# Top-k attention and a SwiGLU block on one core: the penalty of the scores left out comes from ScalarE's Relu instead of VectorE's comparison

## The chip, the core and the metric

The kernel runs on one core of a Trainium2 chip. The metric is device time in microseconds (us) of one execution; lower is better. Five engines work side by side, each in the order of its own queue: TensorE (PE; its weight loads are listed as PEld), VectorE (DVE), ScalarE (ACT), GpSimd (POOL) and SyncE (SP, which issues the DMAs here). An engine that meets an instruction whose input is not there waits, and everything behind it in its queue waits too.

## The reference, cut to what matters

```python
# q, k, v: 8 batches x 8 heads x 576 x 64
scores = scale * np.matmul(q, k.transpose(0, 1, 3, 2))
kth = np.partition(scores, -32, axis=-1)[..., -32:-31]
scores = np.where(scores >= kth, scores, -1000000000.0)
attn = np.exp(scores - scores.max(-1, keepdims=True))
attn = attn / (attn.sum(-1, keepdims=True) + 1e-09)
x = (attn @ v)                      # then to 4608 tokens x 512
g = x @ w_gate                      # 512 -> 1536
out = (g * sigmoid(g) * (x @ w_val)) @ w_out
```

Each row of 576 scores keeps its 32 largest; the others get a weight of zero. Everything is float32.

## The kernel before, in words

**Units.** The attention is cut into 160 units, one for a batch, a block of queries and a pair of heads. Of a batch's five query blocks, four have 128 rows, and their units hold two heads as two halves of 576 columns (128 such units in all). The fifth has 64 rows, and its units pack both heads into one 128-row tile of 576 columns (32 "half units", four in a row at the end of each batch).

**What a unit goes through.** `scores` (L278): PE multiplies queries and keys into PSUM banks (four for a full unit, two for a half one; L308, L294), and ACT copies them to the tile `sc` (L313, L299). `select` (L316): DVE finds the 32 largest of each row with four `max` of eight each into `m` (L328) and three `match_replace` that take the found ones out (L332, working copy `e`). Then DVE writes the penalty into `e`: 0 where the score is at least the 32nd largest, -3e38 elsewhere (L338). `penalize` (L342): POOL computes `bias` from the row's largest (L348) and adds `sc` to the penalty in `e` (L350). `weigh` (L353): ACT takes the exponential of `e` with its row sums (L359), and adds a small constant to them (L364). `normalize` (L367): DVE takes the reciprocal of the sums (L371), ACT multiplies (L374). `turn` (L376): PE transposes `e` through PSUM (L386), ACT copies it to `et` (L387). `values` (L397): PE multiplies with v (L420), ACT copies into the block `xT` (L436).

**The second half.** Each 256 tokens whose `xT` is complete make a block of `feed` (L462; 18 blocks): PE products with the gate and value weights (L476); ACT applies tanh, a scaling and a shift, or copies (L501 to L503, L508); POOL multiplies (L504, L509). The output product is done in seven quarter products (L562), fed by sums and differences that POOL forms (L569, L577, L582, L610) and collected by ACT copies (L589, L596, L639, L651) and POOL adds (L548). Block 0 uses a plain product (L522). The weights are rounded on the way in by ACT, DVE and POOL (L114 to L123) in the first fifth of the span.

**The order of the work.** It is written out by hand in one loop over the units (L747), and each engine keeps it: L818 to L830 tie every instruction to the one before it on its engine. In round n of the loop, in this order: ACT work left over from `feed`; `penalize(n-1)`; POOL work left over; the ACT part of `normalize(n-2)`; `scores` of unit n+1 (even rounds only, which do two units' scores); `values` of two units (even rounds); the matmuls of the second `scores`; `weigh(n-1)`; the copies of the second `scores`; then `select(n)` on DVE, with pieces of `feed` on PE, `turn(n-2)` and the preparation of later batches' keys and queries (L248) between its steps; at its end the reciprocal of `normalize(n-1)`. How many pieces of `feed` a round gets is fixed when the program is built, by a budget of 7.0 (later 6.4) per full unit less a charge for the other matmuls (`share`, L694).

```python
        flush(on_act)
        if 0 <= n - 1 < NU:
            penalize(n - 1)
        flush(on_pool)
        run(scaled)
        if nxt:
            run(nxt.pop(0))
```

**Buffers.** `sc` and `e` have three buffers, `m` two. The PSUM pool for scores, transposes and value products has five banks (`ps_t`, L86), so that the second scores of an even round need the banks of the first; `feed` has three (`ps_f`).

Of the kernel before, what the change touches and what calls it, by code (L numbers as in the profile page):

```python
# [8 lines left out]
AF = mybir.ActivationFunctionType  # L9
ALU = mybir.AluOpType  # L10
FP32 = mybir.dt.float32
# [4 lines left out]
P = 128  # L16
TOP_K = 32
LOWEST = -3.4028234663852886e38
FAR = -3.0e38
EPS = 1.0e-9  # L20
BLK = 256
WP = 256
# [3 lines left out]
def kernel(  # L26
# [37 lines left out]
    nc = tc.nc  # L64
# [11 lines left out]
    scale = 1.0 / float(D) ** 0.5  # L76
# [6 lines left out]
    small = ctx.enter_context(tc.tile_pool(name="small", bufs=3))  # L83
# [190 lines left out]
    def n_heads(qt):  # L274

        return 1 if qt == J else 2
# [39 lines left out]
    def select(n):  # L316

        nh = n_heads(units[n][1])
        sc = state[n]["sc"]
        m = small.tile([P, 2, TOP_K], FP32, tag="m", name="m", bufs=2)  # L320
        heads = [slice(t * S, (t + 1) * S) for t in range(nh)]
        e = work.tile([P, 2 * S], FP32, tag="e", name="e", bufs=3)
        state[n] |= dict(m=m, e=e, heads=heads)
        cur = sc
        rounds = TOP_K // 8
        for r in range(rounds):
            for t, hs in enumerate(heads):
                nc.vector.max(m[:, t, 8 * r : 8 * r + 8], cur[:, hs])  # L328
                yield
            if r < rounds - 1:  # L330
                for t, hs in enumerate(heads):
                    nc.vector.match_replace(  # L332
                        e[:, hs], m[:, t, 8 * r : 8 * r + 8], cur[:, hs], LOWEST
                    )
                    yield
                cur = e
        for t, hs in enumerate(heads):
            nc.vector.tensor_scalar(  # L338
                e[:, hs], sc[:, hs], m[:, t, TOP_K - 1 : TOP_K], FAR, ALU.is_lt, ALU.mult
            )  # L340

    def penalize(n):  # L342

        st = state[n]
        sc, m, e, heads = st.pop("sc"), st.pop("m"), st["e"], st["heads"]
        nh = len(heads)
        bias = small.tile([P, 2], FP32, tag="bias", name="bias")
        nc.gpsimd.tensor_scalar_mul(bias[:, 0:nh], m[:, 0:nh, 0], -scale)  # L348
        for hs in heads:
            nc.gpsimd.tensor_tensor(e[:, hs], e[:, hs], sc[:, hs], ALU.add)  # L350
        st["bias"] = bias

    def weigh(n):  # L353
# [393 lines left out]
    for n in range(NU + 3):  # L747
        nh = n_heads(units[n][1]) if n < NU else 1
        topk = select(n) if n < NU else no
        norm = normalize(n - 1) if 0 <= n - 1 < NU else no  # L750
        nxt = [scores(m) for m in scored(n)]
# [16 lines left out]
        if 0 <= n - 1 < NU:  # L768
            penalize(n - 1)
# [90 lines left out]
```

## Time and profile before

| | |
|---|---|
| three runs | 1786.62, 1790.91, 1791.84 us; median 1790.91 |
| the profiled execution | 1790.76 us, of it a span of 1788.7 us from the first to the last instruction |
| mean granted TensorE clock | 0.966 of full speed |
| instructions | 30860 |

The profile's page gives for each engine its busy time and the number of its instructions, then the same in 40 equal slices of the span as tenths (one slice is 44.7 us), then groups of instructions: line, engine, operation, output and inputs with shapes, count, then the busy time of the group, the mean ns of one, and the idle time just before them with what ended it. Views of the trace give the same for any stretch, instruction by instruction (timeline), or as sums by stretch (windows).

### The profile page before, as it was taken

How to read it: one execution, taken by the hardware profiler on the slowest of the kernel's cores; microseconds unless marked ns; L12 is line 12 of the kernel's file. 1: busy time of each engine (PE TensorE's matmuls, PEld its weight loads, DVE VectorE, ACT ScalarE, POOL GpSimd, SP SyncE). 2: the span in 40 equal slices, each digit the busy share in tenths (PEclk: the TensorE clock that was granted, in tenths of full speed). 3: DMA queues.
4: the chain of work that ended last, by engine and by line, in shares of the span. 5: the costliest groups of instructions: out<-in, count | busy, mean ns of one | idle time of the engine just before them, and what ended most of it. 6: DMA issues, size and time to landing. Idle time of an engine off the chain costs nothing.

```text
span 1788.7 us, 30860 instructions
## 1 busy us (share of the span) xinstructions
PE 1686.3 (94%) x11012; PEld 1396.2 (78%) x11012; DVE 1619.7 (91%) x3372; ACT 1209.5 (68%) x2881; POOL 1068.0 (60%) x1058
## 2 busy tenths in 40 slices
PE   4458999799999999999999999999999999999999
PEld 3337678588888888888888878888888878888877
DVE  7999999999999999999999989999999999999400
ACT  6788776667667677667666776767676776676431
POOL 4878856455565646564656646566556555756434
PEclk7669999899999999999999999999999999999989
DMA  7433030001200030001200030000300020000000
GB/s 193 126 96 95 32 75 14 13 1 36 60 1 13 3 80 15 12 1 35 62 13 1 13 71 26 1 13 6 90 1 13 1 55 15 13 1 13 1 12 12
DMA packets 109306, 59.67 MB, mean 33 GB/s; under 512 B 88544, under 2 KB 96992, under 8 KB 109152
## 3 DMA queue, kind: packets, MB, share of 16 engines
q1 hardware_dynamic: 108016, 57.37, 12.3%
q8 instruction: 87, 1.43, 0.3%
q14 instruction: 67, 0.55, 0.1%
q10 hardware_dynamic: 1136, 0.33, 0.1%
HBM read 48.23 MB, written 9.44 MB: 32 GB/s over the span
## 4 chain that ended last, share of the span: by engine, by line
PE 81%; DVE 9%; POOL 4%; ACT 3%; issue 2%; DMA 0%; SPq 0%; POOLq 0%; ACTq 0%; DVEq 0%
PE f L476 39%; PE x_ps L562 9%; PE av L420 8%; PE s L308 7%; PE etps L386 6%; PE y_ps L562 6%; DVE m L328 4%; DVE e L332 4%; PE s L294 2%; POOL e L350 1%; PE kqps L263 1%; PE o_ps L522 1%; DVE e L338 1%; DVE size L121 1%; ACT e L359 1%
## 5 line engine op out<-in xcount | busy, mean ns | idle before, releaser
L328 DVE MAX8 m<-e 128x8 f32<-128x576 f32 x864 | 614.5, 746 | 3.3
L350 POOL TENSOR_TENSOR e<-e,sc 128x576 f32<-128x576 f32 x288 | 408.7, 1437 | 111.8 <-DVE e L338 53.8
L332 DVE MATCH_REPLACE8 e<-m,e 128x576 f32<-128x576 f32 x576 | 423.3, 741 | 0.0
L476 PE MATMUL f<-xT,wg 128*128 128x256 f32 x1728 | 405.6, 384 | 0.0
L476 PE MATMUL f<-xT,wv 128*128 128x256 f32 x1728 | 399.6, 380 | 0.0
L476 PEld LDWEIGHTS f<-xT,wg 128*128 128x128 f32 x1728 | 326.4, 192 | 52.2 <-issue 8.9
L476 PEld LDWEIGHTS f<-xT,wv 128*128 128x128 f32 x1728 | 323.0, 190 | 49.1 <-issue 7.9
L504 POOL TENSOR_TENSOR h<-h,half_g 128x512 f32<-128x512 f32 x108 | 139.0, 1287 | 284.1 <-ACT h L503 274.5
L359 ACT ACTIVATE e<-e,bias 128x576 f32<-128x576 f32 x288 | 222.8, 778 | 79.0 <-POOL e L350 79.0
L509 POOL TENSOR_TENSOR h<-h,val 128x512 f32<-128x512 f32 x108 | 139.4, 1291 | 148.7 <-ACT val L508 147.9
L386 PE MATMUL etps<-ident,e 128*128 128x128 f32 (+1 forms) x1312 | 184.0, 284 | 45.7 <-ACT e L374 37.5
L374 ACT ACTIVATE e<-e,tot 128x576 f32<-128x576 f32 x288 | 210.9, 781 | 20.9 <-DVE tot L371 20.8
L308 PE MATMUL s<-kqT 64*128 64x288 f32 x1024 | 181.4, 461 | 41.9 <-ACT sc L313 27.6
L386 PEld LDWEIGHTS etps<-ident,e 128*128 128x128 f32 (+1 forms) x1312 | 157.5, 145 | 76.6 <-ACT e L374 41.4
L387 ACT COPY et<-etps 128x512 f32<-128x512 f32 (+1 forms) x448 | 182.5, 483 | 44.1 <-PE etps L386 44.0
L332 DVE MATCH_REPLACE8 e<-m,sc 128x576 f32<-128x576 f32 x288 | 211.5, 740 | 0.0
L328 DVE MAX8 m<-sc 128x8 f32<-128x576 f32 x288 | 202.5, 739 | 9.1 <-ACT sc L313 9.1
L338 DVE TENSOR_SCALAR e<-sc,m 128x576 f32<-128x576 f32 x288 | 185.4, 680 | 1.1
L313 ACT COPY sc<-s 128x288 f32<-128x288 f32 x512 | 164.9, 407 | 17.0 <-PE s L308 16.8
L308 PEld LDWEIGHTS s<-kqT 64*128 64x128 f32 x1024 | 102.6, 198 | 89.6 <-ACT sc L313 33.0
L420 PE MATMUL av<-et,v 128*64 128x128 f32 (+1 forms) x2560 | 158.6, 267 | 0.0
L501 ACT ACTIVATE h<-f 128x512 f32<-128x512 f32 x108 | 64.3, 595 | 116.8 <-PE f L476 116.6
(73 smaller groups left out, 2045.9 us busy)
## 6 DMA issues: line engine op xcount, KB each, us to landing
v<-in_v_dram SPq DMA_DIRECT2D x32, 256.0 KB, 3.2
kq_in<-in_k_dram SPq DMA_DIRECT2D x63, 128.0 KB, 2.9
kq_in<-in_q_dram SPq DMA_DIRECT2D x63, 128.0 KB, 3.1
w<-in_moe_w_gate_dram SPq DMA_DIRECT2D x12, 512.0 KB, 3.9
w<-in_moe_w_val_dram SPq DMA_DIRECT2D x12, 512.0 KB, 3.7
w<-in_moe_w_out_dram SPq DMA_DIRECT2D x12, 512.0 KB, 3.6
out_dram<-o SPq DMA_DIRECT2D x38, 128.0 KB, 2.4
out_dram<-o SPq DMA_DIRECT2D x16, 256.0 KB, 2.4
```

Source lines behind the costliest of these rows:

```text
L308: nc.tensor.matmul(ps[:, 0:half], slab[d, q0 : q0 + P], slab[d, k0 : k0 + half])
L328: nc.vector.max(m[:, t, 8 * r : 8 * r + 8], cur[:, hs])
L332: nc.vector.match_replace(e[:, hs], m[:, t, 8 * r : 8 * r + 8], cur[:, hs], LOWEST)
L338: nc.vector.tensor_scalar(e[:, hs], sc[:, hs], m[:, t, TOP_K - 1 : TOP_K], FAR, ALU.is_lt, ALU.mult)
L350: nc.gpsimd.tensor_tensor(e[:, hs], e[:, hs], sc[:, hs], ALU.add)
L359: nc.scalar.activation(e[:, hs], e[:, hs], AF.Exp, bias=bias[:, t : t + 1], scale=scale, accum_out=tot[:, t : t + 1],)
L374: nc.scalar.mul(e[:, hs], e[:, hs], tot[:, t : t + 1])
L386: nc.tensor.transpose(ps[0:kl, c * P : (c + 1) * P], e[:, k0 : k0 + kl], ident[:])
L387: nc.scalar.copy(et[0:kl, c0 : c0 + cn, :], ps[0:kl, 0 : cn * P].rearrange("p (c j) -> p c j", c=cn),)
L420: nc.tensor.matmul(av[d, i, 0:ql], weights_, moving, start=c == (0 if last else J), stop=c == (J if last else J - 1),)
L476: nc.tensor.matmul(ps[:, i, :], w[:, kc, m * P : (m + 1) * P], x[:, kc, :], start=(kc == 0), stop=(kc == KC - 1),)
L562: nc.tensor.matmul(ps, lhsT, T[i][m], start=m == 0, stop=m == MQ - 1)
```

## The change

`select` no longer writes the penalty. `penalize` now has ACT scale the 32nd largest by 2^110 into a small tile `top`, compute `Relu(-2^110 * score + top)` into `e` for each head (0 for the scores kept, a very large number for the others), and has POOL subtract that from the scores. The subtraction of a huge number takes the place of the addition of -3e38.

```diff
-FAR = -3.0e38
+BIG = 2.0**110
...
                 cur = e
-        for t, hs in enumerate(heads):
-            nc.vector.tensor_scalar(
-                e[:, hs], sc[:, hs], m[:, t, TOP_K - 1 : TOP_K], FAR, ALU.is_lt, ALU.mult
-            )
 
     def penalize(n):
...
         nh = len(heads)
+        top = small.tile([P, 2], FP32, tag="top", name="top")
+        nc.scalar.mul(top[:, 0:nh], m[:, 0:nh, TOP_K - 1], BIG)
         bias = small.tile([P, 2], FP32, tag="bias", name="bias")
         nc.gpsimd.tensor_scalar_mul(bias[:, 0:nh], m[:, 0:nh, 0], -scale)
-        for hs in heads:
-            nc.gpsimd.tensor_tensor(e[:, hs], e[:, hs], sc[:, hs], ALU.add)
+        for t, hs in enumerate(heads):
+            nc.scalar.activation(
+                e[:, hs], sc[:, hs], AF.Relu, bias=top[:, t : t + 1], scale=-BIG
+            )
+            nc.gpsimd.tensor_tensor(e[:, hs], sc[:, hs], e[:, hs], ALU.subtract)
         st["bias"] = bias
```

## The prediction

> **What bounds the kernel now.** I read the page's busy shares first, then the slices, then the windows by stage.
>
> ```profile
> PE 1686.3 (94%) x11012; PEld 1396.2 (78%) x11012; DVE 1619.7 (91%) x3372; ACT 1209.5 (68%) x2881; POOL 1068.0 (60%) x1058
> ...
> PE   4458999799999999999999999999999999999999
> ...
> DVE  7999999999999999999999989999999999999400
> ```
>
> Two engines look full. The slices part them: in the first four (to 180 us) DVE is full and PE half idle; after that both are full; at the end DVE is done and PE still works. So the windows decide (columns: the stretch, its length, busy us and count of PE, PEld, DVE, ACT, POOL, then granted clock, DMA share, GB/s):
>
> ```profile
> 45.00:90.00 45.00, 21.72 (x138) 15.90 (x138) 45.00 (x92) 34.75 (x76) 37.12 (x31) 0.61 0.44 125
> 90.00:135.00 45.00, 23.57 (x147) 16.25 (x143) 45.00 (x93) 35.60 (x80) 34.80 (x29) 0.63 0.34 95
> ...
> 320.00:500.00 180.00, 168.29 (x1142) 138.77 (x1141) 176.24 (x376) 123.87 (x307) 95.05 (x97) 0.96 0.11 27
> 500.00:800.00 300.00, 298.71 (x1995) 252.09 (x1995) 294.60 (x617) 210.05 (x505) 184.94 (x188) 1.00 0.07 19
> ...
> 1100.00:1400.00 300.00, 298.39 (x1984) 250.57 (x1982) 289.57 (x610) 207.29 (x499) 177.20 (x179) 1.00 0.08 20
> ```
>
> From 500 us on PE is busy 99.5% of the time and DVE 97 to 98%: PE is the bound, with DVE close behind. Only two stretches wait for DVE: the start, and 328 to 355 us, where the second half has no finished tokens and PE stands idle for 11.5 us (sum of its five gaps in the timeline there). PE's work is not touched by the change. So most of what DVE saves cannot shorten the span, but each wait that ACT or POOL puts on PE after 180 us lengthens it at once.
>
> **What is removed.** The groups (count, then busy us and mean ns of one, then idle before):
>
> ```profile
> L350 POOL TENSOR_TENSOR e<-e,sc 128x576 f32<-128x576 f32 x288 | 408.7, 1437 | 111.8 <-DVE e L338 53.8
> ...
> L359 ACT ACTIVATE e<-e,bias 128x576 f32<-128x576 f32 x288 | 222.8, 778 | 79.0 <-POOL e L350 79.0
> ...
> L374 ACT ACTIVATE e<-e,tot 128x576 f32<-128x576 f32 x288 | 210.9, 781 | 20.9 <-DVE tot L371 20.8
> ...
> L338 DVE TENSOR_SCALAR e<-sc,m 128x576 f32<-128x576 f32 x288 | 185.4, 680 | 1.1
> ```
>
> L338 goes: 288 instructions, 185.4 us of DVE. A pair that nothing disturbs takes 0.93 us (timeline at 906 and 916 us), so a full unit of DVE falls from 10.6 to 9.6 us, while PE needs 11.2 (a pair of rounds repeats every 22.4 us). Single ones range from 490 to 1611 ns with a median of 512. The Trainium skill, "SBUF — State Buffer", section Who interferes with whom, says that a VectorE `tensor_scalar` in a two-port mode and GpSimd lock each other out; the spread of L338 fits, and by it POOL would win back something too. The rows bound that: L350 has a mean of 1437 ns and a minimum of 1396, so at most 288 x 41 ns = 12 us of an engine that is 60% busy. I count nothing for it.
>
> **What is added.** No Relu is in the trace. Its nearest row is L374: same shape, same engine, a scale per row; a pair takes 1.44 us. The copy behind it starts about 0.1 us before its end, so 1.34 us of queue. `top` on 128x2 is like L364 (296 ns for 128x2 in the groups by form); Relu reads its result, so all of it counts, with some hand-over. Bounds: 0.2 + 1.34 and 0.3 + 2 x 0.78. I take 1.7 us for a full unit and 1.1 for a half one: 128 x 1.7 + 32 x 1.1 = 253 us of queue, and ACT goes from 1209 to about 1460 us, 82%. The instruction order of the new program holds one table load on ACT, as before, so no reload is added.
>
> The Trainium skill, "ScalarE: Activation LUTs", Rules for kernel authors, speaks against the move: relu and mul belong on VectorE. Its formula (280 ns + 0.833 ns per element with a pointer for the bias) gives 760 ns for one Relu, as L374 has; its rule ignores which engine has room, and by its price the sum below would stay.
>
> **Where it stands.** In round n the new ACT work comes after what `feed` left on ACT and ahead of L374 and the copies of the first scores. Those copies free the PSUM banks in which PE wants to write the second scores. ACT waited for DVE's end at this place already (for the reciprocal), so no wait of a new kind arises on ACT; the 1.7 us are what is new. POOL's L350 now waits for the Relu instead of L338. One even round as it is now:
>
> ```profile
> 918.69 1.24 PE L308 MATMUL s<-kqT 64*128 64x288 f32 x8
> 918.80 0.60 ACT L501 ACTIVATE h<-f 128x512 f32<-128x512 f32 x1 [2.08 <-PE f L476]
> ...
> 919.77 0.63 ACT L503 ACTIVATE h<-h 128x512 f32<-128x512 f32 x1
> ...
> 920.29 1.44 ACT L374 ACTIVATE e<-e,tot 128x576 f32<-128x576 f32 x2
> ...
> 921.62 1.29 ACT L313 COPY sc<-s 128x288 f32<-128x288 f32 x4
> ...
> 922.20 1.07 PEld L308 LDWEIGHTS s<-kqT 64*128 64x128 f32 x8 [0.17 <-ACT sc L313]
> ```
>
> ACT's chain starts when PE ends a product (918.8), so an earlier DVE does not help it. PE reaches the second scores at 922.2 and waits 0.17 us for the first copy. With 1.7 us put in before L374, PE stands still about 1.7 us here, and this comes back whenever the gate's three operations are left over.
>
> **The sum**, from 180 to 1660 us, slack by slack in the timeline:
> - Second scores. Slack is from the end of the first copy to PE's need; ACT's idle time before that copy adds to it, and the last copies trail by 0.2. Of 56 even rounds with two heads, 33 cover 1.7 us; 4 lack 0.6, 10 about 0.8, 2 about 1.4, and 7 the whole 1.7: 2.4 + 8 + 2.8 + 11.9 = 25 us. Of 14 half rounds, 5 lack about 0.25: 1. Together **+26**.
> - Transposes (L386) after L374 in odd rounds. Of 57, 2 have 0.05 us of slack and 10 have 0.75 to 1.0: 2 x 1.65 + 10 x 0.8 = 11; three half ones lack 0.45. **+12**.
> - Half units. From 1044 to 1060.5 us, in three rounds, ACT is busy 14.4 of 16.5 us; 3 x 1.1 more makes 17.7, over the length. That is 1.2 us at least, and some waits stay: 1.5 x 7 batches, **+10**.
> - POOL's L350 now begins at the Relu's end, in places 1.6 to 2.7 us later than now. In three blocks (301, 1066 and 1526 us) the differences of L569 follow it closely, with PE 0.05 us behind; two more lack 0.4. **+7**.
> - The PSUM banks of `feed` have 3.6 us of slack or more between products (L476): nothing. ACT's wait for L350 before the exponentials (57 us from 300 to 1600 us) is mostly filled by the new work; that is why odd rounds cost no more.
> - 328 to 355 us: DVE saves 0.93 us in three rounds, and can come in some 5 us early, from the rounds before, in which PE was the bound. **-8**, between 0 and -18 (11.5 of idle, and half of the 13.7 us at half clock that the clock records show beside it).
> - The start: about 13 units to 180 us. DVE would save 13 x 1.1 = 14. But ACT is busy 66.6 of 80 us between 100 and 180, which is 10.4 of a unit's 12.5; 1.7 more makes 12.1, and it waits 28 us there for weight transfers, 2.1 a unit. If these waits shrink as ACT comes later, there is a gain of 5; if they stay, a loss of 13 x 1.7 = 22. I take **0**, between -14 and +22.
> - Small waits of PE on DVE's or POOL's lateness elsewhere: **-3**.
>
> 26 + 12 + 10 + 7 - 8 - 3 = +44. The sum is made against the profiled execution's 1790.76 us (span 1788.7, 2.1 around it), which lies 0.15 us under the median: **1835 us**.
>
> **Rivals.**
> - *Faster.* DVE's room is used and the covers hold: once DVE leads by up to 5 us, ACT does the Relu in time in which it waits now (it idles 580 us of the span), so that no bank comes late. What is left is the start and the stretch at 328: 14 + 17, **1760 us**. For it: DVE is full to 180 us, and 33 of 56 even rounds have cover. It decides if the waits added stay under the 31 us won. Against it: ACT's chain starts from PE's product, not from DVE.
> - *Nothing to measure* (about 5 us, 0.3%, is what a measurement can tell): losses of some 10 us meet gains of 10, **1791**.
> - *ACT as the bound.* Every even round loses the full amount and the half units saturate: 57 x 1.7 + 16 x 1.1 = 115, less 26, with the start at +22: 44 + 89 + 22, about **1945 us**; half of that already is over 1880. For it: from 860 to 1036 us ACT is busy 120.2 of 176 us, 15.3 of a pair of rounds; 3.4 more makes 84%. Against it: the rounds with 2.4 us of slack, in which ACT waits for PE.
> - That the change does not do what it says can be excluded: the new order has no L338 on DVE.
>
> **How the numbers follow.** Forecast, 1796 to 1880: 0.69. Nothing to measure: 0.08. Faster: 0.14, part of it just under 1785. ACT as the bound, over 1880: 0.09. Faster 0.14, same 0.08, slower 0.78. The range reaches from 1779 to 1880; it leaves out the bulk of the faster case and the last one, some 0.2.
>
> **What would show it.** Right: DVE down by about 185 us with idle time inside, ACT up by about 250; PE idle after 180 us in many gaps of 0.5 to 2 us before the second scores, ended by the copies L313, and before transposes, ended by L374; windows of half units longer by 1 to 2 us. Wrong: PE still at 99% from 500 to 1400 us; or a first stage ending well before 180 us; or PE gaps mainly in places that I gave cover (the products of `feed`).

## The result, and the profile after

| | before | after |
|---|---|---|
| median | 1790.58 us (4 runs, 1786.62 to 1791.84) | 1854.24 us (4 runs, 1852.13 to 1857.83) |
| profiled execution, its span | 1790.76, 1788.7 us | 1854.77, 1853.0 us |
| DVE, ACT, POOL busy | 1619.7, 1209.5, 1068.0 us | 1451.5, 1422.0, 1042.8 us |

The change makes the kernel slower: the ratio is 1.0361, with a 95% interval of 1.0338 to 1.0385, 64 us. The page of after, its busy shares and its PE and DVE slices (a slice is now 46.3 us):

```profile
PE 1706.3 (92%) x11012; PEld 1408.0 (76%) x11012; DVE 1451.5 (78%) x3084; ACT 1422.0 (77%) x3329; POOL 1042.8 (56%) x1058
...
PE   4448999799999999999999999999999999999999
...
DVE  6986788997888978887888878887988879888300
```

DVE has lost its fullness everywhere, the start included, and PE is no fuller for it. The windows of after show where PE lost:

```profile
45.00:90.00 45.00, 23.95 (x144) 16.67 (x141) 41.19 (x87) 39.01 (x87) 33.27 (x28) 0.59 0.40 113
90.00:135.00 45.00, 19.00 (x96) 13.62 (x97) 37.56 (x80) 41.24 (x90) 31.92 (x28) 0.60 0.34 105
...
320.00:500.00 180.00, 164.43 (x1114) 134.67 (x1113) 156.88 (x334) 142.44 (x345) 95.89 (x102) 0.96 0.11 27
500.00:800.00 300.00, 292.79 (x1938) 245.19 (x1937) 255.96 (x545) 240.95 (x566) 167.75 (x174) 1.00 0.08 19
1100.00:1400.00 300.00, 288.80 (x1916) 241.51 (x1917) 250.98 (x536) 236.06 (x564) 164.85 (x173) 0.99 0.10 26
```

From 500 to 800 and from 1100 to 1400 us PE was busy 99.5% and is now busy 97.6 and 96.3%. The granted clock does not account for it: it is 0.99 to 1.00 in these windows, and by the clock records the stretches at half clock after 180 us sum to 27 us in both kernels. In the first stage ACT has taken DVE's part: from 90 to 135 us ACT is busy 41.2 of 45 us, DVE 37.6. The waits of PE in after from 180 to 1720 us (what PE waited for: us in total, times, longest):

```profile
PE s L308 <- ACT sc L313: 21.0, 21, 4.0
PE etps L387 <- ACT e L375: 12.2, 15, 3.4
PE x_ps L563 <- POOL xT L570: 6.7, 3, 2.7
PE s L308 <- ACT et L388: 6.4, 6, 2.3
PE kqps L263 <- ACT et L388: 4.9, 3, 2.0
PE s L294 <- ACT sc L313: 4.1, 2, 2.7
```

In before the same list, over the same stretch, begins:

```profile
PE etps L386 <- ACT e L374: 11.8, 4, 5.3
PE s L308 <- ACT sc L313: 4.3, 2, 3.6
PE x_ps L562 <- POOL xT L569: 2.7, 2, 2.2
```

The places that grew are those that were forecast: score matmuls that wait for the copies, transposes that wait for ACT's multiplication (L374 before, L375 now), the first quarter products behind POOL. For the transposes it is the number of waits that grew (from 4 to 15), not their sum. The even round that the prediction showed, in after:

```profile
957.09 1.24 PE L308 MATMUL s<-kqT 64*128 64x288 f32 x8
...
957.20 0.60 ACT L502 ACTIVATE h<-f 128x512 f32<-128x512 f32 x1 [2.07 <-PE f L477]
...
958.68 0.21 ACT L344 ACTIVATE top<-m 128x2 f32<-128x2 f32 x1
...
958.92 1.44 ACT L348 ACTIVATE e<-sc,top 128x576 f32<-128x576 f32 x2
...
960.27 1.43 ACT L375 ACTIVATE e<-e,tot 128x576 f32<-128x576 f32 x2
...
961.60 1.27 ACT L313 COPY sc<-s 128x288 f32<-128x288 f32 x4
...
962.03 1.19 PEld L308 LDWEIGHTS s<-kqT 64*128 64x128 f32 x8 [1.61 <-ACT sc L313]
```

From `top` to L375 pass 1.59 us (958.68 to 960.27; 1.7 was taken), and the second scores, which had waited 0.17 us, wait 1.61.

**A view made from two traces.** The 11012 matmuls come in the same order in every kernel here. So the k-th matmul's start in one trace, less its start in the trace of before, says how late PE is at each point of the work, and the growth of this between two matmuls says at which line it was lost. This measure is used for all runs below (us; "at 180" is the point that PE passed at 180 us in before; in the 5 us behind that point some runs shift by 1 to 3 us, so these figures are no finer than that):

| | late at 180 us | added from there | at the end |
|---|---|---|---|
| after | +13.1 | +51.1 | +64.2 |

Of the 51.1, the score matmuls L308 hold 29.4, the half units' L294 4.9, the preparation of keys 3.2, the transposes 9.7, the quarter products `x_ps` 6.1; the products of `feed` and the value products come out 1 us shorter each.

### The profile page after: what moved, and what is told of

Its sections match the earlier page's. It is cut to its first block, busy times and chain, and to the rows that moved or that the text cites. A ratio compares the mean times of both kernels' runs of the same rounds, so it can differ in the third digit from the quotient of the medians.

```text
span 1853.0 us, 30964 instructions
## 1 busy us (share of the span) xinstructions
PE 1706.3 (92%) x11012; PEld 1408.0 (76%) x11012; DVE 1451.5 (78%) x3084; ACT 1422.0 (77%) x3329; POOL 1042.8 (56%) x1058
## 4 chain that ended last, share of the span: by engine, by line
PE 72%; ACT 17%; POOL 6%; DVE 1%; issue 1%; DMA 1%; SPq 1%; ACTq 0%; POOLq 0%
PE f L477 36%; PE x_ps L563 9%; PE s L308 6%; PE av L421 6%; PE etps L387 6%; PE y_ps L563 6%; ACT e L348 4%; POOL e L351 3%; ACT e L375 2%; PE s L294 2%; ACT e L360 1%; ACT sc L313 1%; ACT et L388 1%; PE o_ps L523 1%; ACT size L114 1%
## 5 line engine op out<-in xcount | busy, mean ns | idle before, releaser
L351 POOL TENSOR_TENSOR e<-sc,e 128x576 f32<-128x576 f32 x288 | 402.7, 1417 | 345.5 <-ACT e L348 345.5
L360 ACT ACTIVATE e<-e,bias 128x576 f32<-128x576 f32 x288 | 222.8, 779 | 48.9 <-POOL e L351 45.7
L308 PE MATMUL s<-kqT 64*128 64x288 f32 x1024 | 192.2, 470 | 68.6 <-ACT sc L313 49.6
L348 ACT ACTIVATE e<-sc,top 128x576 f32<-128x576 f32 x288 | 209.4, 769 | 5.2
L375 ACT ACTIVATE e<-e,tot 128x576 f32<-128x576 f32 x288 | 206.9, 760 | 0.0
L308 PEld LDWEIGHTS s<-kqT 64*128 64x128 f32 x1024 | 113.9, 200 | 116.6 <-ACT sc L313 58.5
L372 DVE RECIPROCAL tot<-tot 128x2 f32<-128x2 f32 (+1 forms) x160 | 25.0, 156 | 196.8 <-ACT tot L365 196.8
```

The lines of the kernel that those rows point to most:

```text
L308: nc.tensor.matmul(ps[:, 0:half], slab[d, q0 : q0 + P], slab[d, k0 : k0 + half])
L348: nc.scalar.activation(e[:, hs], sc[:, hs], AF.Relu, bias=top[:, t : t + 1], scale=-BIG)
L351: nc.gpsimd.tensor_tensor(e[:, hs], sc[:, hs], e[:, hs], ALU.subtract)
L360: nc.scalar.activation(e[:, hs], e[:, hs], AF.Exp, bias=bias[:, t : t + 1], scale=scale, accum_out=tot[:, t : t + 1],)
L375: nc.scalar.mul(e[:, hs], e[:, hs], tot[:, t : t + 1])
```

## The experiments

The theory: the loss is made by 1.6 us of Relu work a full unit in ScalarE's queue ahead of L374 and the first score copies, and by what stands behind the held subtraction in GpSimd's. The rivals: GpSimd's wait alone; ScalarE's load, wherever it stands. "After" below is the changed kernel, "before" the kernel before; ratios are to runs of before on the same chip. A dash in the diffs is taken out, a plus is put in.

### What VectorE's room is worth alone

```diff
 (before)
-        for t, hs in enumerate(heads):
-            nc.vector.tensor_scalar(
-                e[:, hs], sc[:, hs], m[:, t, TOP_K - 1 : TOP_K], FAR, ALU.is_lt, ALU.mult
-            )
```

> The kernel before without the comparison L338 and with nothing in its place: the penalty is left out, so weights are not limited to the 32 largest; everything else runs as before (POOL still adds sc to e). It shows what VectorE's room alone is worth. Theory (after 180 us PE is the bound, and the change costs time only by the Relu in ScalarE's queue): only the start and the stretch at 328 to 355 us gain, 10 to 25 us, so 1765 to 1780. Rival (VectorE's room is of no use even there, since ScalarE and the weight transfers hold the start): 1785 to 1791.

Measured: 1765.87 us, ratio 0.986 (0.9845 to 0.9875). PE is 14.9 us early at 180 us, gains 5.4 more between 330 and 360 us, and 3.8 near 1060 us. So the room is worth 25 us when nothing is paid for it, and almost nothing of it lies in the stages in which PE is full. That is the ceiling for any change that only takes this comparison off DVE and leaves the order as it is, as against 185 us of removed DVE time.

### The Relu added, nothing removed

```diff
 (before, in penalize)
+        top = small.tile([P, 2], FP32, tag="top", name="top")
+        nc.scalar.mul(top[:, 0:nh], m[:, 0:nh, TOP_K - 1], 2.0**110)
+        for t, hs in enumerate(heads):
+            spare = work.tile([P, S], FP32, tag="spare", name="spare", bufs=1)
+            nc.scalar.activation(
+                spare[:], sc[:, hs], AF.Relu, bias=top[:, t : t + 1], scale=-(2.0**110)
+            )
```

> The kernel before, complete, plus the same scaling and the same Relu on ScalarE in the same place, written to a spare tile that nobody reads; VectorE's comparison and GpSimd's addition stay as they were. Theory (the cost is the 1.6 us a full unit put into ScalarE's queue ahead of L374 and the first score copies): the loss of the change comes back nearly whole without GpSimd being held, 1840 to 1860, with the delay of PE against the kernel before growing at the score matmuls and transposes. Rival (the cost is GpSimd's subtraction, which now waits 345 us for the Relu): no more than 15 us of loss, 1790 to 1806. If VectorE being full adds to it: over 1860.

Measured: 1837.57 us, ratio 1.0264 (1.0244 to 1.0284); PE +3.3 at 180 us, +46.2 from there, of which the score matmuls L308 28.2 and the transposes 13.8, and the quarter products -3.5. It is 2.4 us under the expected range, because the start does not lose 13 us here. After 180 us the Relu in ScalarE's queue makes 46 us here, against the 51 of after, with GpSimd not held (41 in the run that also drops the comparison, below). So GpSimd's wait cannot be the main cause of those.

### The same work, earlier in the queue

```diff
 (after: top and the Relu moved out of penalize into distance)
         next(norm, None)
         scaled = norm
+        if n < NU:
+            distance(n)
         pieces(6)
```

> The changed kernel with the scaling and the Relu of unit n issued on ScalarE at the end of round n, ahead of the last pieces of the second half, instead of at the head of round n+1; GpSimd's subtraction stays where it is. Same work on every engine. Theory (place in the queue): the waits of PE for second scores and transposes after 180 us go, and 35 to 45 of the 54 us lost there come back: 1805 to 1820; the start may stay 13 us late. Rival (ScalarE's load of 77% in total is the cost, wherever it stands): 1845 or more. A new wait could take its place: ScalarE waits for VectorE's end of unit n ahead of the gate's operations; then DVE m is named as releaser of ScalarE's idle time.

Measured: 1823.49 us, ratio 1.0189 (1.0173 to 1.0204); +13.1 at 180 us as in after, +19.8 from there in place of 51.1. At the score matmuls L308 9.5 us are left of 29.4, at the transposes 4.3 of 9.7. ScalarE does the same work, so 31 us of the 51 belong to its place. GpSimd's subtraction is still held here, by 33.4 us from 20 to 180 us against 34.0 in after, and the start loses the same 13.1. The total is 3.5 us over the expected range. ScalarE waits 15.1 us for DVE m before `top` after 180 us: the wait that could take the old one's place is there, and small.

### The same work, later in the queue

```diff
 (after)
         flush(on_act)
-        if 0 <= n - 1 < NU:
-            penalize(n - 1)
         flush(on_pool)
         run(scaled)
         if nxt:
             run(nxt.pop(0))
+        if 0 <= n - 1 < NU:
+            penalize(n - 1)
```

> The changed kernel with the whole of penalize(n-1) moved behind normalize(n-2) and the first scores of the round, so that L374 and the first score copies go ahead of the Relu; GpSimd's subtraction then comes later, and the exponentials wait for it. Same work on every engine. Theory (place in the queue): the second scores and the transposes of odd rounds are free again, some 35 us come back, less a few for exponentials that wait 1 to 2 us a round: 1810 to 1830. Rival (total load): 1845 or more.

Measured: 1899.16 us, ratio 1.0599 (1.0581 to 1.0616); +20.8 at 180 us, +89.6 from there: 45 us worse than after, where a gain of some 30 was expected. Two groups show it, the exponentials (L360) of after and of this run, with the idle time before them at the end of the line:

```profile
L360 ACT ACTIVATE e<-e,bias 128x576 f32<-128x576 f32 x288 | 222.8, 779 | 48.9 <-POOL e L351 45.7
```

```profile
L360 ACT ACTIVATE e<-e,bias 128x576 f32<-128x576 f32 x288 | 223.2, 775 | 196.8 <-POOL e L351 196.2
```

The exponentials now stand right behind the Relu whose subtraction they need, ScalarE sits idle for it in nearly every unit, and everything behind them is late: of the delay added after 180 us, 28.4 us come at the quarter products, 16.0 at the preparation of keys, 16.1 at transposes and 9.8 at value products, most of it at places that lost less or nothing in after. I had put "a few us" on this wait; it is 196 us of ScalarE's time. The run does not yet say whether the place before the copies matters here, so the wait was taken away next.

### The late place without the wait for GpSimd

```diff
 (after's work, GpSimd unheld: before without L338; the Relu to the tile spare in distance)
         if nxt:
             run(nxt.pop(0))
+        if 0 <= n - 1 < NU:
+            distance(n - 1)
```

> As the run with GpSimd unheld (no comparison, the Relu to a spare tile, GpSimd adds sc to e at its old place; the penalty is left out), with the scaling and the Relu moved behind L374 and the first score copies, as in the run with the late Relu. That one lost 108 us where a gain of some 30 was expected; its exponentials waited 179 us for GpSimd. Theory (the wait for GpSimd made that loss; the place behind the copies itself is good): the exponentials no longer wait, and second scores and odd transposes are free: 1775 to 1800, faster than the 1824 of the unheld run with the Relu in front. Rival (ScalarE is too full for the Relu anywhere in the first half of a round): 1824 or more.

Measured: 1782.80 us, ratio 0.9947 (0.993 to 0.9963); PE 8.3 us early at 180 us, +2.9 from there. ScalarE does all of the new work here, 223.4 us of Relu, and the kernel is faster than before. Against the run with VectorE's room alone, which ends at 1765.87 us, the Relu costs 17 us in this place (20 between the two profiled executions, 13.4 of them after 180 us: +2.9 against -10.5). Those 13.4 at most are left for the load as the cause after 180 us. It also lays the loss of the late run on the wait for GpSimd. By which way, this run does not part: the exponentials no longer wait for GpSimd, and GpSimd's own queue, behind which the quarter products stood, no longer waits for the Relu. (It is no usable kernel: the penalty is left out.)

### ScalarE's work in front, GpSimd unheld

```diff
 (before without L338, and with the spare Relu of "The Relu added")
```

> The change's VectorE saving and its ScalarE work, but without holding GpSimd: no comparison L338, the Relu goes to a spare tile, and GpSimd adds sc to e as in the kernel before (the penalty is left out, the weights are not limited to 32). Theory of the start (the change is 13 us late at 180 us mainly because GpSimd's subtraction waits for the Relu and holds the rounding of the weights behind it, whose buffers ScalarE waits for): PE is at most 3 us late at 180 us, and the whole is 1825 to 1840, with the waits at second scores still there. Rival (ScalarE's own load holds the start): 8 us or more late at 180 us, and 1845 to 1860.

Measured: 1824.05 us, ratio 1.0194 (1.0179 to 1.0208); 1 us under the expected range; PE is 5.5 us early at 180 us, +41.4 from there. At 180 us, then: 15 us early with DVE's room alone, 5.5 early with the Relu too, 13.1 late when GpSimd's subtraction waits for the Relu. ScalarE's load takes 9.4 us of the room, and the held subtraction 18.6 more. After 180 us the held subtraction makes 51.1 - 41.4 = 9.7 us, as much as the quarter products differ (-4.5 here and +6.1 in after); what the other places gain and lose by it about cancels.

### One head

```diff
 (after; the comparison L338 is kept for heads[0], and GpSimd adds there)
+        if nh == 2:
+            nc.scalar.mul(top[:, 0:1], m[:, 1, TOP_K - 1 : TOP_K], BIG)
...
+            if t == 0:
+                nc.gpsimd.tensor_tensor(e[:, hs], e[:, hs], sc[:, hs], ALU.add)
+                continue
             nc.scalar.activation(
-                e[:, hs], sc[:, hs], AF.Relu, bias=top[:, t : t + 1], scale=-BIG
+                e[:, hs], sc[:, hs], AF.Relu, bias=top[:, 0:1], scale=-BIG
             )
```

> The changed kernel with the Relu for the second head of a full unit alone; the first head and the half units keep VectorE's comparison and GpSimd's addition. ScalarE's new work in front of L374 is then about 0.9 us a full unit instead of 1.6, and none in half units. Theory (slack by slack): only rounds with less than 0.9 us of slack lose: second scores 2 x 0.6 + 7 x 0.9 = 8 us, transposes 2 us, half units nothing; VectorE's half saving gives back up to 7 at the start: 1788 to 1802, far less than half of the change's 64. Rival (a cost that goes with the amount of ScalarE work): about half of 64, 1815 to 1830.

Measured: 1800.27 us, ratio 1.0061 (1.0047 to 1.0075). PE is 0.9 us early at 180 us and loses 9.9 from there: 8.2 at the score matmuls, 1.0 at the transposes, where the slacks gave 8 and 2. Half of the full units' new work costs 10 us, not half of 64: a cost in slack is not in proportion to the work.

### One head, early

```diff
 (the run before, with top and the Relu in distance)
         next(norm, None)
         scaled = norm
+        if n < NU:
+            distance(n)
         pieces(6)
```

> As the run with one head, with the Relu issued at the end of the unit's own round, ahead of the last pieces of the second half. Theory (slack): the 10 us at second scores and transposes go as well, and VectorE's half saving at the start and at 328 to 355 us is left, if ScalarE and GpSimd let it through: 1780 to 1791, perhaps faster than both kernels. Rival (amount of work): 1810 or more.

Measured: 1788.08 us (11 runs, 1784.18 to 1789.36) against 1790.67, ratio 0.9985 (0.9976 to 0.9993). It leaves nothing of the reference's work out, and it beats both kernels, after by 66 us and before by some 2.6: 0.07 to 0.24%. PE is 1.1 us early at 180 us and gains 3.2 from there.

### The start: is it GpSimd's fullness?

The held subtraction in after, GpSimd's timeline:

```profile
101.26 0.21 POOL L346 TENSOR_SCALAR bias<-m 128x2 f32<-128x2 f32 x1
106.62 2.97 POOL L351 TENSOR_TENSOR e<-sc,e 128x576 f32<-128x576 f32 x2 [5.15 <-ACT e L348]
109.55 1.57 POOL L122 TENSOR_TENSOR size<-size,w 128x512 int32<-128x512 int32 x1
111.19 1.28 POOL L123 TENSOR_TENSOR wg<-size,w 128x512 f32<-128x512 f32 x1
112.44 1.28 POOL L122 TENSOR_TENSOR size<-size,w 128x512 int32<-128x512 int32 x1
113.79 1.29 POOL L123 TENSOR_TENSOR wv<-size,w 128x512 f32<-128x512 f32 x1
115.04 1.29 POOL L122 TENSOR_TENSOR size<-size,w 128x512 int32<-128x512 int32 x1
116.40 1.30 POOL L123 TENSOR_TENSOR wv<-size,w 128x512 f32<-128x512 f32 x1
```

GpSimd waits 5.15 us for the Relu and then works off three pieces of weight rounding that stand behind; their buffers take the next weight transfers, for which ScalarE waits. From 20 to 180 us ScalarE's idle time before L114 (transfers, and GpSimd's L122) is 22.7 us in after and 5.4 us in the unheld run. That alone proves little, since it is 26.3 us in before, where DVE was full and nobody missed ScalarE. What is new in after is that DVE waits for ScalarE's part (L121 behind L114): 22.6 us from 20 to 180 us, 12.2 in the unheld run, nothing in before. Two pairs of runs take the rounding off GpSimd:

```diff
 (e9 from before, e10 from after)
-        nc.gpsimd.tensor_tensor(bits, bits, low, ALU.add)
 (e11 from before, e12 from after: this too, and the weights set to 0.01)
-        nc.gpsimd.tensor_tensor(dst, size[:], high, ALU.mult)
```

> The kernel before without the addition L122 in the rounding of the weights on GpSimd (the low part of the rounding is left out), a base for the next run: 36 x 1.3 = 47 us less GpSimd work in the first 180 us. VectorE is full there, so PE should pass 180 us within 3 us of the kernel before, 1785 to 1793.

> The changed kernel without the addition L122 on GpSimd (the low part of the rounding is left out). Theory of the start (13 us late because the subtraction, held by the Relu, holds the rounding behind it in a GpSimd queue that is then too full): with 47 us less in that queue PE is at most 5 us late at 180 us against the base run without L122, and the whole comes to 1838 to 1848. Rival (any wait of the subtraction for the Relu costs this, however full GpSimd is): 10 us late or more, 1850 or more.

Measured, one run each: 1776.12 and 1846.54 us. The base is 13.0 us early at 180 us, which I had not expected (see the last section). Against it the changed kernel is 17.5 us late at the point that the base passed at 180 us (16.1 at the point of the table), no better than 13.1. So the queue's fullness is not what makes the held subtraction dear; that part of the theory falls, though the total came within its range.

> The kernel before without both GpSimd operations in the rounding of the weights (L122 and L123); the weights are set to a constant instead, and the products are not the reference's. It is the base for the next run: 12 to 18 us early at 180 us against the kernel before, as the run without L122 was 13 us early, or later by what the 18432 constants a partition cost GpSimd at the very start.

> The changed kernel without L122 and L123 in the same way. Nothing of the rounding now stands behind the held subtraction in GpSimd's queue, and the weight buffers come free when ScalarE has done its part. Theory of the start, in what is left of it (the held subtraction delays the rounding behind it in order, whose buffers the next weight transfers and so ScalarE wait for): ScalarE's idle time before L114 for weight transfers or GpSimd is under 5 us from 20 to 180 us (23 in the changed kernel), and PE is no later at 180 us than 4 us against the base without L122 and L123. Rival (the held subtraction delays the start through something else, the exponentials or ScalarE's own queue): 9 us late or more at 180 us. After 180 us both: some 50 us are lost as in the changed kernel.

Measured, one run each: 1772.90 and 1834.18 us. The base is 14.6 us early at 180 us. The changed kernel is 8.3 us late against it at the point that the base passed at 180 us, and 5.6 at the point of the table (9.0 early against before). ScalarE's wait for weight transfers is 5.2 us, down from 22.7 and just over the 5 that were expected. So without rounding behind the held subtraction the start is no later than in the unheld run (5.5 early against before). That speaks for the chain held subtraction, rounding, buffers, transfers, ScalarE. It does not settle it: 5.6 and 8.3 lie between the two expectations, and the base gained 14.6 from the same edit by another way. Nor does it say what bounds the start now. From 45 to 135 us ScalarE is busy 89.5 of 90 us, but VectorE is busy 90.0, and its shift in the rounding takes longer than in the base, although each does 20 of them there. First the base, then the changed kernel, from 45 to 135 us:

```profile
L123 DVE TENSOR_SCALAR size<-size 128x512 int32<-128x512 int32 x20 | 8.1, 403 | 0.0
```

```profile
L123 DVE TENSOR_SCALAR size<-size 128x512 int32<-128x512 int32 x20 | 14.4, 719 | 0.0
```

That is 6.3 us, about as much as the lateness. VectorE slowed beside GpSimd (last section) is a rival to ScalarE's load in this pair, and no run parts the two.

## Why the prediction was right, and where its sizes were off

The direction, the mechanism and the range held: 1835 was forecast, 1854 measured, within 1779 to 1880.

- **What bounds the kernel.** Right. 25 us of a removal of 185 are worth anything, and they lie at the start and at 328 to 355 us, with 3.8 near 1060 us that were not foreseen (first experiment).
- **The new work on ScalarE.** Taken 1.7 us a full unit, measured 1.59; ACT rose by 213 us, not 250: busy time counts an overlap once, and neighbours overlap by about 0.1 us. One Relu takes 769 ns by the groups of after, close to L374's price as assumed (781 before, 760 after). DVE fell by 168 us, not 185.
- **Second scores, +26, and half units, +10.** Measured at L308, L294 and the preparation of keys: 29.4 + 4.9 + 3.2 = 37.5. Put by the prediction's own parts, the second scores of full units lost 23.4 us (25 forecast), those of half units 4.9 (1), and the seven stretches of half units at the ends of batches grew by 9.4 (10), 1.9 of it counted already. It is right round by round too: of the 56 even rounds 30 lost under 0.2 us, where 33 had been given cover, and 6 lost the whole 1.6, where 7 had been expected to. With the Relu behind the copies (the late run with GpSimd unheld) none of the 56 loses 0.2 us.
- **Transposes, +12.** Measured 9.7.
- **GpSimd's delay at the quarter products, +7.** Measured 6.1; against a kernel with GpSimd unheld, where they are 4.5 us early, it is 10.6.
- **328 to 355 us, -8.** Mis-sized: PE's lateness falls only from 21.1 us (at 320) to 19.7 (at 400), 1.4. Without the Relu the same stretch gives 5.7 (13.7 to 19.4 early at 500). The likely reason is that PE waits there for DVE's end and the Relu now stands between that end and L374. It is not the whole one: with the Relu behind L374 (the late run with GpSimd unheld) the stretch gives 3.0.
- **The start, 0 between -14 and +22.** The term that was mis-sized most: +13.1. ScalarE's 83% from 100 to 180 us was read rightly; the 28 us of waits for transfers belong to the whole start (26.3 from 20 to 180 us), since from 100 to 180 us ScalarE idles 13.4 us in all. But the price of the room lost was taken from ScalarE alone. The runs put ScalarE's load at 9.4 and the held subtraction at 18.6, against 14.9 of room. That GpSimd's add is first in a queue with the weights' rounding was in the view of before, and I priced it only after 180 us. The 0 itself was a choice between a gain and a loss that no row had settled.
- **The rivals.** "Faster" fails where it was said to: ScalarE's chain starts at PE's product. "ScalarE as the bound" can hold for the start alone (41.2 of 45 us in after, 89.5 of 90 in the last run, though VectorE is as full in the latter); after 180 us the late unheld run does all of the work for 2.9 us more than before.

The Trainium skill, "ScalarE: Activation LUTs", Rules for kernel authors, which gives relu to VectorE, had the sign right here, for another reason than its own. A Relu costs 769 ns and an undisturbed comparison 0.5 us, but the runs show that the place in the queue counts for more than this price. Measured against the run with VectorE's room alone (1765.87 us), the full Relu work costs 88 us in front of L374, 58 at the end of the round before, and 17 behind the first copies, where nobody waits for its result.

## What to carry to other kernels

When two engines look full, ask which of them PE or the last stage waits for, and take the ceiling of a change from there: here 25 us for 185 us of removed work. Work moved to an engine with room is paid for by what stands behind it in that engine's queue: list the slack of each consumer, add the new time, and count only what goes over; that gave 8 and 2 us for one head where 8.2 and 1.0 were measured. If a second engine's operation has to wait for the moved one, price what stands behind that too, and move producer and consumer apart in the order before giving the change up.

## What the hardware showed that was not expected

VectorE's `tensor_scalar` gets slower beside GpSimd, and its `max` does not. From 20 to 180 us, the comparison, the shift of the rounding (L121 in before, L123 in the run without GpSimd's rounding) and `max`, in before:

```profile
L328 DVE MAX8 m<-e 128x8 f32<-128x576 f32 x77 | 54.8, 744 | 0.0
...
L121 DVE TENSOR_SCALAR size<-size 128x512 int32<-128x512 int32 x31 | 21.0, 679 | 0.0
L338 DVE TENSOR_SCALAR e<-sc,m 128x576 f32<-128x576 f32 x26 | 19.6, 794 | 0.0
```

and with GpSimd's rounding operations gone:

```profile
L328 DVE MAX8 m<-e 128x8 f32<-128x576 f32 x82 | 58.1, 741 | 0.0
...
L123 DVE TENSOR_SCALAR size<-size 128x512 int32<-128x512 int32 x34 | 15.4, 454 | 0.0
L338 DVE TENSOR_SCALAR e<-sc,m 128x576 f32<-128x576 f32 x28 | 14.6, 558 | 0.0
```

The comparison falls from 794 to 558 ns, the shift from 679 to 454, `max` stays at 744 and 741. DVE was busy 90 of 90 us from 45 to 135 in both, and the start became 14.6 us shorter: part of that fullness was waiting. By the counts, 26 x 236 + 31 x 225 ns = 13 us. In the run without L122 alone, where the two take 592 and 521 ns, the same working gives 10 us for a start that is 13.0 early. Within the one trace of before it shows as well: over the whole span the 169 comparisons with a GpSimd instruction beside them take 801 ns on average and the 119 without one 508, while `max` takes 744 and 746. The Trainium skill, "SBUF — State Buffer", section Who interferes with whom, says that `tensor_scalar` in a two-port mode and GpSimd block each other for whole instructions, and that an instruction with one SBUF input outside those modes does not contend; these rows agree, though no run shows in which mode the comparison ran.
